# A gated complex scan with a gated feed-forward layer: the third group's running sums taken as whole 4-byte products, and three planner constants with early values

## The chip, the cores and the metric

The kernel runs on one core of one Trainium2 chip. The metric is the device time of one execution in microseconds (us), shown as the median of repeated runs. Before the change it is 616.79 us, the median of 3 runs that lie between 616.0 and 617.45.

## The reference

Inputs are `q`, `k`, `v`, `a_re` and `a_im` of shape 4 x 8 x 768 x 48 (batch, heads, time, width) and three weight matrices in 8-byte floats, 384 x 1536 twice and 1536 x 384. Cut to what matters:

```python
scale = np.minimum(mag, 0.999) / (mag + 1e-06)      # mag = |a|
for t in range(S):
    S_re, S_im = ar*S_re - ai*S_im + kv, ar*S_im + ai*S_re
    y[:, :, t] = einsum('bhd,bhde->bhe', q[:, :, t], S_re)
x = y.transpose(0, 2, 1, 3).reshape(B * S, H * D)   # 3072 x 384
g = x @ w_gate
out = (g * sigmoid(g) * (x @ w_val)) @ w_out
```

## The kernel before, in words

Time is cut into 6 chunks of 128 steps. A chunk of one batch is a slab (24 in all), and two slabs of the same chunk are a group (12, numbered 0 to 11). Each group has two halves of work.

**The scan side** (`stage_ops`, `pair_ops`). The decay of a step is turned into the logarithm of its size and its phase. Both are summed over the 128 steps of a slab by one product with a triangular matrix on TensorE (`cumulate`, L458 to 473; `cumL` sums the logarithms, `cumF` the phases). Exponentials, cosine and sine of the sums scale and turn `q` and `k`; then come scores, a mask, the product with `v` and the state that is carried on. The result is `xh` and `xl`, the rounded feed-forward input and its remainder.

**The feed-forward side** (`ffn_ops`). For each of 12 column blocks there are the products L897 (gate and value, into `p_gv`), a SiLU on ScalarE (L907), a product on VectorE (L912), and the output product L936 (into `p_po`). Group 0 takes these as whole 4-byte products, because its weights are only just converted; groups 1 to 11 take three rounded products each, of a high and a low part of both operands (type fp32r). VectorE converts the 8-byte weights in groups of three instructions (L792, L796, L800) and then splits them (L326 or L328 rounds, L322 subtracts).

**How a running sum is taken.** In groups 0 and 1 (`exact = g < 2`) `cumulate` issues one 4-byte product for each slab (L469), which runs as two TensorE instructions. From group 2 on it first calls `split`: a rounding cast (planned on VectorE or ScalarE) and a subtraction (VectorE or GpSimd) over 128 x 768 values, and then two fp32r products for each slab (L472). Since `cumulate` is called twice in a group, a split group has two casts, two subtractions and eight products; an exact group has eight TensorE instructions and no cast. The split parts borrow buffers: `LATER` puts the high and low logarithm into the buffers `s2` and `re`, those of the phase into `s1` and `s2`. For that reason the dictionary `held` (L367) makes the next group's loads and squares wait for `ls1` and `lim`, the subtractions.

**The order of the work** is not written by hand. `Planner.plan` is a list scheduler that runs when the program is built. Every operation has a key, its due time: given by `anchor` for scan slabs, by `T0`, `FT0`, `T1` and `FT` for feed-forward blocks, and handed back to what it depends on (`urge`). Whenever an engine is free in the plan, the ready operation with the smallest rank goes next. The rank is the key, plus `SWITCH_KEY` for an activation that needs another table, plus `YIELD` for an operation that VectorE could leave to another engine. `AHEAD` shifts the due times of the scan slabs. The engines then run their queues strictly in that order; before the planned time `WARM` TensorE is kept going with products of no use (L1037). `CONV0`, `CK0` and `X_SEC` give due times to weight conversions and to checks of the inputs' range.

Of the kernel before, what the change touches and what calls it, by code (L numbers as in the profile page):

```python
# [30 lines left out]

SWITCH = 1.273
HOP = 0.145
SWITCH_KEY = 2.93
STRETCH = 1.636
AHEAD, YIELD, QUEUED = -3.449, 3.533, 4.228
T0, PER, FT, FT0 = 11.002, 21.487, 3.599, 4.531
LEAD0, LEAD2 = 14.347, -0.647
CONV0, CONVP = 136.292, 171.866
T1 = T0 + 12 * FT0  # L40
CK0, CKP = 795.217, 26.993
WARM, CLEAR = 36.0, 12.0
ROW, LAND = 0.6, 2.4
SPARE, PIECE, CHECK = 0.85, 0.826, -0.265
X_SEC = 430.022
RCP, SQR, TURN, SEC = 1, 2, 4, 4
HIGH, LOW, WHOLE = 0, 1, 2
SHY = -80.37
POOL_FROM = 134.7
JOIN = 4  # L50

# [13 lines left out]
class Planner:  # L67
# [21 lines left out]
    def urge(self):  # L89
# [3 lines left out]
        for op in reversed(self.ops):  # L93
            for d in op.deps:
                span = STRETCH * max(d.engs.values()) + (0.5 * SWITCH if d.table else 0.0) + d.lat + d.move + HOP
                d.key = min(d.key, op.key - span)

    def plan(self):
        self.urge()
        free = {e: 0.0 for op in self.ops for e in op.engs}  # L100
        held = {tag: [] for tag in self.slots}
        tables, moved, shut = set(TABLES["ln"]), 0.0, 0.0
        followers, missing = {}, {}
        for op in self.ops:
            missing[op] = len(set(op.deps))
            for d in set(op.deps):
                followers.setdefault(d, []).append(op)
        loads = []
        left, order = [op for op in self.ops if not missing[op]], []
        while left:  # L110
            ready = {e: [] for e in free}
            for op in left:
                t = max([d.end + HOP for d in op.deps], default=0.0)
                for tag, _ in op.alloc:
                    if len(held[tag]) >= self.slots[tag]:
                        rel = self.released(tag, held[tag][0])
                        if rel is None:
                            t = None
                            break
                        t = max(t, rel)  # L120
                if t is None:
                    continue
                if op.move:
                    t = max(t, moved - QUEUED)
                for e in op.engs:
                    if e == "POOL" and len(op.engs) > 1 and t < POOL_FROM:
                        continue
                    ready[e].append((max(t, shut) if op.port and e in ("DVE", "POOL") else t, op))
            def rank(op):
                sw = e == "ACT" and op.table and not tables & set(TABLES[op.table])  # L130
                other = e == "DVE" and len(op.engs) > 1
                return op.key + (SWITCH_KEY if sw else 0.0) + (YIELD if other else 0.0), op.idx

            pick = None
            for e, c in ready.items():
                if c:
                    when = max(free[e], min(t for t, _ in c))
                    if e == "POOL":

                        op = min((o for t, o in c if t <= when + 0.02), key=rank)  # L140
                        if any(o.port and t <= when + 0.02 and o.key + SHY < op.key for t, o in ready.get("DVE", ())):
                            continue
                        when -= 1e-6
                    if pick is None or when < pick[0]:
                        pick = (when, e)
            if pick is None:
                raise RuntimeError("nothing can go on: " + ", ".join(o.name for o in left))
            when, e = pick
            op = min((o for t, o in ready[e] if t <= when + 0.02), key=rank)
            cost = op.engs[e]  # L150
            if e == "ACT" and op.table:

                if not tables & set(TABLES[op.table]):
                    tables = set(TABLES[op.table])
                    loads.append((op, tables))
                    cost += SWITCH
                else:
                    tables &= set(TABLES[op.table])
            for tag, inst in op.alloc:
                if len(held[tag]) >= self.slots[tag]:  # L160
                    held[tag].pop(0)
                held[tag].append(inst)
            op.start, op.eng = when, e
            free[e] = when + cost
            op.end = when + cost + op.lat
            if op.port and e in ("DVE", "POOL"):
                shut = when + cost
            if op.move:
                moved = max(moved, when + cost + 0.6) + op.move
                op.end = moved + op.lat  # L170
            order.append(op)
            left.remove(op)
            for o in followers.get(op, ()):
                missing[o] -= 1
                if not missing[o]:
                    left.append(o)
        for op, tables in loads:
            op.load = min(tables)
        return sorted(order, key=lambda o: (o.start, o.idx))


def flat(t):
    return t.rearrange("p h d -> p (h d)")
# [10 lines left out]
def quick(ctx, tc, q, k, v, a_re, a_im, w_gate, w_val, w_out, out, count):  # L194
# [81 lines left out]
    for t, (nm, f, i) in {"re": ("w", 0, 0), "im": ("w", 0, 1), "s1": ("o", 0, 0), "s2": ("w", 1, 0), "s3": ("w", 1, 1),  # L276
                          "qt": ("o", 1, 0), "kt": ("o", 2, 0), "qs": ("w", 2, 0)}.items():
        n, nm_f = 96 if t == "qs" else D, (nm, NF - 3 + f)
# [9 lines left out]
    pl = Planner(slots)  # L288
# [49 lines left out]
    def anchor(n):  # L338
        if n < 2:
            return T0 - LEAD0 + 3.0 * n  # L340
        if n < 4:
            return T0 + 4.0 + (n - 2) * 6 * FT0 - LEAD2
        return T1 + 4.0 + (n - 4) * PER - AHEAD


    def stage_ops(g, first, many):
        N = str(g) if many == 2 else f"{g}{'ab'[first]}"
        c, bp = divmod(g, 2)
        exact, lent = g < 2, g == 0
# [3 lines left out]
        def tg(t):  # L353
            at = LATER.get(t, t)
            return (("lent", at, first) if lent and t != "ks" else at), (t, g)
# [37 lines left out]
        for x, t in (("r", "s1"), ("i", "s2")):  # L393
            def square(e, x=x, t=t):
# [3 lines left out]
                else:  # L398
# [3 lines left out]
                   deps=[{"r": "ld_re", "i": "ld_im"}[x] + N, held.get(name, "")], alloc=[tg(t)], use=[tg({"r": "re", "i": "im"}[x])])  # L402
# [27 lines left out]
        def ratio(e):  # L430
            if divided:
                nc.vector.scalar_tensor_tensor(out=of("im"), in0=of("im"), scalar=-1.0, in1=of("s3"), op0=ALU.mult, op1=ALU.mult)
            else:
                nc.vector.scalar_tensor_tensor(out=of("im"), in0=of("re"), scalar=2.0, in1=of("im"), op0=ALU.subtract, op1=ALU.mult)
        pl.add("ratio" + N, STT, ratio, deps=["rec" + N, "sqi" + N] if divided else ["e1" + N, "b1" + N],
               use=[tg("s3" if divided else "re"), tg("im")], port=True)
# [20 lines left out]
        bank = "gv" if g == 0 else "pm"  # L457

        def cumulate(name, t, after):
            ins = [tg(t)]  # L460
            if not exact:
                after, ins = split(t, after)
            for i in slabs:
                inst = f"{name}{g}.{i}"

                def fn(e, i=i, inst=inst):
                    ps = new(bank, inst)[:, :HD]
                    if exact:
                        nc.tensor.matmul(out=ps, lhsT=mask, rhs=flat(half(t, i)), start=True, stop=True)  # L469
                    else:  # L470
                        for j, x in enumerate(("h" + t, "l" + t)):
                            nc.tensor.matmul(out=ps, lhsT=tri, rhs=flat(half(x, i)), start=j == 0, stop=j == 1)  # L472
                pl.add(inst, {"PE": 0.7 if exact else 0.37}, fn, deps=[after], alloc=[(bank, inst)], use=ins)

        cumulate("cumL", "s1", "l2" + N)
        for i in slabs:
            inst = f"cumL{g}.{i}"

            def exps(e, i=i, inst=inst):
                if i == first:  # L480
# [6 lines left out]
                   alloc=[] if i > first else [tg("qs")], use=[(bank, inst)] + ([tg("qs")] if i > first else []), table="exp")  # L487
        scaled = [f"exps{g}.{i}" for i in slabs]
        if c < NCH - 1:
# [6 lines left out]
            def dr2(e):  # L496
                dec = at_["dec", g] if first else new("dec", g)
                for j in range(2):
# [3 lines left out]
                   alloc=[] if first else [("dec", g)], use=[("dec", g)] if first else [], lat=5.0 if exact else 3.0 + SPARE)  # L502
# [9 lines left out]
        if c > 0:  # L512
            def cy(e):
                s = new(*tg("s"))
                for i, nm in enumerate(before):
# [3 lines left out]
                   alloc=[tg("s")], lat=2.5 + SPARE, move=1.1)  # L519
        cumulate("cumF", "im", "at" + N)  # L520
        for i in slabs:
            inst = f"cumF{g}.{i}"

            def total(e, i=i, inst=inst):
# [7 lines left out]
                else:  # L532
                    nc.vector.scalar_tensor_tensor(out=s, in0=ps, scalar=INV_2PI, in1=s, op0=ALU.mult, op1=ALU.add)
            pl.add(f"sadd{g}.{i}", STT1 if c else {"DVE": 0.47, "ACT": 0.42}, total,
                   deps=[inst, "cy" + N, "e1" + N, "b1" + N] + ([f"sadd{g}.{first}"] if i > first else []),
                   alloc=[tg("s")] if c == 0 and i == first else [],
                   use=[(bank, inst)] + ([] if c == 0 and i == first else [tg("s")]))
# [18 lines left out]
        for dst, t in (("ks", "kt"), ("qs", "qt")):  # L556
            for j, (cs, w) in enumerate(((slice(0, D), "u"), (slice(D, 96), sine))):
                opens = dst == "ks" and j == 0 and first == 0
                after = [] if opens or dst == "qs" else [f"ks0_{g}a" if first else "ks0_" + N]

                def turn(e, dst=dst, t=t, cs=cs, w=w, opens=opens):
                    if opens:
# [3 lines left out]
                       deps=["cos" + N if j == 0 else "sin" + N, "qtm" + N, "ktm" + N] + (["dr1" + N] if dst == "qs" else []) + after,  # L566
                       alloc=[tg(dst)] if opens else [], use=[tg(t), tg(w)] + ([] if opens else [tg(dst)]))
# [10 lines left out]
    def slab_ops(n):  # L578
# [81 lines left out]
        scored = dict(deps=tdeps + [f"sc{n - 1}"], alloc=[("ps", f"{n}.0"), ("ps", f"{n}.1")], use=[("T", n)])  # L660
        joined = half == 1 and n >= JOIN
        if joined:
# [191 lines left out]
    def sector_ops(g):  # L854

        N, key = f"s{g}", X_SEC + 5.0 * g
        both, parts = [(("wo", x), N) for x in range(2)], [(("ww", x), N) for x in range(2)]
# [360 lines left out]
```

## Time and profile before

| what | value |
|---|---|
| median of 3 runs | 616.79 us (616.0 to 617.45) |
| the profiled execution's own time | 616.11 us |
| its span in the profile | 614.1 us |
| PE (TensorE matmuls) busy | 595.0 us, 97% |
| DVE (VectorE) busy | 490.8 us, 80% |
| ACT (ScalarE) busy | 425.0 us, 69%, of which 119 table loads 152.7 us |
| POOL (GpSimd) busy | 39.5 us, 6% |
| granted TensorE clock, mean | 0.994 of full speed |

The span is the stretch that the profiler records; the execution's own time is 2.0 us longer. A busy share is an average: an engine can be the bound in one stretch and have slack in another, so the stretches below are read one by one. The busy time of PE is modelled for each matmul and overlaps at its ends; what a matmul takes from its engine is read from the distance of its start to the next start. In the rows, a bracket such as [1.11 <-DVE sg L912] is idle time just before the instruction and what ended it.

### The profile page before, as it was taken

What the parts mean: (1) busy time and instruction counts of PE and PEld (TensorE: products, weight loads), DVE (VectorE), ACT (ScalarE), POOL (GpSimd) and SP (SyncE); (2) the same over time, 40 slices, a digit from 0 to 9 for tenths busy, and PEclk for the clock granted to TensorE, in tenths of its full rate; (3) what the DMA queues carried; (4) which work ended last, traced back from release to release, by engine and by line L of the source; (5) the groups of instructions that cost most, each with busy time, mean ns of one, the idle gap of its engine ahead of it and who ended that gap; (6) DMA issues with size and microseconds to landing.
All of it is one profiled execution on the core that took longest, in us unless ns stands there. A gap on an engine that the chain in (4) does not pass through costs nothing.

```text
span 614.1 us, 18072 instructions
## 1 busy us (share of the span) xinstructions
PE 595.0 (97%) x7520; PEld 564.2 (92%) x7520; DVE 490.8 (80%) x892; ACT 425.0 (69%) x691; POOL 39.5 (6%) x70
## 2 busy tenths in 40 slices
PE   8789999999999999999999999999999999999995
PEld 6567778889999999999999999999999999999995
DVE  7999999999999898688688788778878868554442
ACT  7963776996865865995994994995896896213310
POOL 3210101001001000000001001001000000000000
PEclk9989999999999999999999999999999999999998
DMA  9999512443755535536545445544644643541300
GB/s 263 312 309 334 142 51 58 120 104 75 194 134 124 170 88 147 137 95 169 130 108 159 123 117 147 135 112 123 162 113 121 170 112 90 148 105 59 101 24 30
DMA packets 146279, 83.15 MB, mean 135 GB/s; under 512 B 106608, under 2 KB 142448, under 8 KB 146192
## 3 DMA queue, kind: packets, MB, share of 16 engines
q1 hardware_dynamic: 143360, 77.10, 46.7%
q0 software_dynamic: 2256, 4.06, 2.9%
q8 instruction: 61, 1.00, 0.7%
q10 hardware_dynamic: 576, 0.79, 0.4%
q14 instruction: 26, 0.21, 0.1%
HBM read 61.40 MB, written 4.78 MB: 108 GB/s over the span
## 4 chain that ended last, share of the span: by engine, by line
PE 79%; DVE 12%; ACT 4%; issue 2%; DMA 2%; SPq 0%; DVEq 0%
PE p_gv L897 42%; PE p_po L936 22%; PE p_py L701 6%; PE p_ps L658 4%; PE p_pm L707 2%; PE p_pm L472 2%; DVE xl L796 2%; DMA qt<-in_q_dram 1%; DVE ww L322 1%; ACT L1040 1%; DVE xl L792 1%; DVE sg L912 1%; DVE ww L800 1%; DVE s L322 1%; DMA ww<-in_a_re_dram 1%
## 5 line engine op out<-in xcount | busy, mean ns | idle before, releaser
L897 PE MATMUL p_gv<-xh,ww 128*128 128x256 f32 x1596 | 304.1, 288 | 3.3 <-DVE sg L912 2.6
L897 PEld LDWEIGHTS p_gv<-xh,ww 128*128 128x128 f32 x1596 | 255.6, 189 | 10.0 <-DVE sg L912 3.7
L897 PE MATMUL p_gv<-xl,ww 128*128 128x256 f32 x726 | 200.9, 277 | 0.0
L1040 ACT ACT_TABLE_LOAD x119 | 152.7, 1283 | 2.1
L897 PEld LDWEIGHTS p_gv<-xl,ww 128*128 128x128 f32 x726 | 136.4, 188 | 0.1
L936 PE MATMUL p_po<-wo,hh 128*128 128x384 f32 x484 | 124.0, 337 | 0.0
L907 ACT ACTIVATE sg<-p_gv 128x256 f32<-128x256 f32 x144 | 54.5, 384 | 91.3 <-PE p_gv L897 90.3
L912 DVE TENSOR_TENSOR sg<-sg,p_gv 128x256 f32<-128x256 f32 x144 | 59.3, 413 | 62.9 <-ACT sg L907 59.8
L936 PEld LDWEIGHTS p_po<-wo,hh 128*128 128x128 f32 x484 | 81.5, 188 | 1.1 <-issue 0.4
L936 PE MATMUL p_po<-wo,hl 128*128 128x384 f32 x242 | 81.0, 335 | 0.0
L322 DVE TENSOR_TENSOR hl<-sg,hh 128x256 fp32r<-128x256 f32 x132 | 55.0, 421 | 6.1 <-ACT hh L326 0.8
L377 ACT ACTIVATE s<-s 128x768 f32<-128x768 f32 x44 | 37.1, 844 | 12.2 <-DVE s L322 12.0
L936 PEld LDWEIGHTS p_po<-wo,hl 128*128 128x128 f32 x242 | 45.4, 188 | 0.0
L326 ACT CAST hh<-sg 128x256 fp32r<-128x256 f32 x61 | 24.7, 404 | 29.6 <-DVE sg L912 26.5
L701 PE MATMUL p_py<-sc,vt 128*32 128x128 f32 x768 | 38.6, 278 | 0.0
L672 DVE TENSOR_TENSOR sc<-p_ps,tri 128x512 f32<-128x512 f32 x48 | 31.4, 679 | 3.1 <-PE p_py L701 3.1
L658 PEld LDWEIGHTS p_ps<-T 96*32 96x32 f32 x1536 | 28.9, 111 | 5.3 <-issue 2.9
L701 PE MATMUL p_py<-T,G 96*32 96x128 f32 x640 | 33.5, 274 | 0.0
L658 PE MATMUL p_ps<-T 96*32 96x128 f32 (+3 forms) x1536 | 32.4, 235 | 0.0
L322 DVE TENSOR_TENSOR ks<-kt,s 128x768 f32<-128x768 f32 x22 | 21.0, 952 | 6.4 <-PE p_pm L707 6.4
L701 PEld LDWEIGHTS p_py<-sc,vt 128*32 128x32 f32 x768 | 24.5, 112 | 1.6 <-issue 0.8
L328 DVE CAST hh<-sg 128x256 fp32r<-128x256 f32 x71 | 21.1, 300 | 4.8 <-PE p_po L936 1.5
(145 smaller groups left out, 858.7 us busy)
## 6 DMA issues: line engine op xcount, KB each, us to landing
T<-turned SPq DMA_DIRECT2D x240, 64.0 KB, 2.1
wo<-in_moe_w_out_dram SPq DMA_DIRECT2D x24, 384.0 KB, 5.5
vt<-in_v_dram SPq DMA_DIRECT2D x24, 288.0 KB, 4.3
ww<-in_moe_w_gate_dram SPq DMA_DIRECT2D x12, 384.0 KB, 7.7
ww<-in_moe_w_val_dram SPq DMA_DIRECT2D x12, 384.0 KB, 8.6
wo<-in_moe_w_gate_dram SPq DMA_DIRECT2D x12, 384.0 KB, 3.5
wo<-in_moe_w_val_dram SPq DMA_DIRECT2D x12, 384.0 KB, 3.9
re<-in_a_re_dram SPq DMA_DIRECT2D x11, 384.0 KB, 3.7
```

Of the source, the lines that this page charges most:

```text
L322: V[e].tensor_tensor(out=out, in0=a, in1=b, op=op)
L326: nc.scalar.copy(out=out, in_=in_)
L328: nc.vector.tensor_copy(out=out, in_=in_)
L377: nc.scalar.activation(out=of(dst), in_=of(source), func=func, scale=scale, **kw)
L658: nc.tensor.matmul(out=ps[32 * slot:32 * slot + 32, at, 32 * j:P], lhsT=kT[:, h // 2, h % 2, j, :], rhs=qT[:, h // 2, h % 2, j:4, :], star ...
L672: nc.vector.tensor_tensor(out=s.rearrange("p (x h) t -> p x h t", x=2), in0=at_["ps", f"{n}.{qd}"].rearrange("p (x h t) -> p x h t", x=2, ...
L701: nc.tensor.matmul(out=o, lhsT=l, rhs=r, start=opens, stop=closes, tile_position=(0, 32 * slot))
L897: nc.tensor.matmul(out=gv[:, i, :], lhsT=l, rhs=r, start=(m == 0), stop=(m == len(mm) - 1))
L907: nc.scalar.activation(out=new("sg", I), in_=at_["gv", I][:, 0:2 * P], func=AF.Silu)
L912: nc.vector.tensor_tensor(out=sg, in0=sg, in1=at_["gv", I][:, 2 * P:4 * P], op=ALU.mult)
L936: nc.tensor.matmul(out=po, lhsT=l[:, cs], rhs=weight("o", f, part), start=f == 0 and j == 0, stop=f == NF - 1 and j == len(products) - 1)
L1040: nc.scalar.preload_act_table_set(op.load)
```

## The change

`EXACT = 3` is new: `cumulate` takes the 4-byte product for groups 0, 1 and 2, where it did so for 0 and 1. Everything else that depended on `exact` still goes by `g < 2`. Since group 2 has no split, the operations `ls1` and `lim` of group 2 do not exist, and the entries of `held` that name them for group 3 fall away. `SWITCH_KEY`, `YIELD` and `AHEAD` get second values for the early part (`EDGE = 150` in the planner's time for two of them, slabs 4 to 7 for the third), and most other constants of the planner have new values.

```diff
-SWITCH_KEY = 2.93
-STRETCH = 1.636
-AHEAD, YIELD, QUEUED = -3.449, 3.533, 4.228
-T0, PER, FT, FT0 = 11.002, 21.487, 3.599, 4.531
-LEAD0, LEAD2 = 14.347, -0.647
-CONV0, CONVP = 136.292, 171.866
+SWITCH_KEY = 2.986
+STRETCH = 1.645
+AHEAD, YIELD, QUEUED = -2.176, -1.261, 2.216
+T0, PER, FT, FT0 = -16.691, 21.329, 3.598, 4.615
+LEAD0, LEAD2 = 13.87, -1.402
+CONV0, CONVP = 236.777, 147.295
-CK0, CKP = 795.217, 26.993
+CK0, CKP = 835.905, 35.026
-SPARE, PIECE, CHECK = 0.85, 0.826, -0.265
-X_SEC = 430.022
+SPARE, PIECE, CHECK = 1.264, 0.546, 0.877
+X_SEC = 687.988
+EDGE = 150.0
+SWITCH_KEY_E, YIELD_E, AHEAD_E = 2.473, 4.357, -4.549
+EXACT = 3
...
-                return op.key + (SWITCH_KEY if sw else 0.0) + (YIELD if other else 0.0), op.idx
+                late = free["PE"] > EDGE
+                return op.key + ((SWITCH_KEY if late else SWITCH_KEY_E) if sw else 0.0) + ((YIELD if late else YIELD_E) if other else 0.0), op.idx
...
-        return T1 + 4.0 + (n - 4) * PER - AHEAD
+        return T1 + 4.0 + (n - 4) * PER - (AHEAD if n >= 8 else AHEAD_E)
...
-            if not exact:
+            if g >= EXACT:
                 after, ins = split(t, after)
...
-                    if exact:
+                    if g < EXACT:
                         nc.tensor.matmul(out=ps, lhsT=mask, rhs=flat(half(t, i)), start=True, stop=True)
...
-                pl.add(inst, {"PE": 0.7 if exact else 0.37}, fn, deps=[after], alloc=[(bank, inst)], use=ins)
+                pl.add(inst, {"PE": 0.7 if g < EXACT else 0.37}, fn, deps=[after], alloc=[(bank, inst)], use=ins)
```

## Rows read from the trace of the kernel before

**Rows 1.** The page: busy time by engine.
```profile
PE 595.0 (97%) x7520; PEld 564.2 (92%) x7520; DVE 490.8 (80%) x892; ACT 425.0 (69%) x691; POOL 39.5 (6%) x70
```

**Rows 2.** Stretches: length, busy us of PE, PEld, DVE, ACT, POOL; clock, DMA.
```profile
62.00:80.00 18.00, 18.00 (x79) 14.13 (x78) 18.00 (x31) 11.64 (x16) 2.03 (x2) 1.00 0.43 108
80.00:101.20 21.20, 20.76 (x221) 16.46 (x220) 21.20 (x37) 15.96 (x25) 2.68 (x4) 1.00 0.21 53
101.20:142.00 40.80, 38.21 (x452) 35.57 (x453) 39.27 (x72) 36.10 (x56) 2.57 (x4) 1.00 0.39 98
142.00:600.00 458.00, 457.41 (x6085) 448.82 (x6076) 352.28 (x653) 316.23 (x524) 20.17 (x33) 1.00 0.48 124
```

**Rows 3.** The chain that ended last, 131 to 134 us: start, us, what.
```profile
131.40 0.34 DVE sg L912
...
131.79 2.32 PE p_gv L897 x18
```

**Rows 4.** Timeline of TensorE: the four idle spots between 62 and 142 us.
```profile
89.62 1.62 PE L936 MATMUL p_po<-wo,sg 128*128 128x384 f32 x4 [0.44 <-DVE sg L912]
...
111.59 0.39 PE L897 MATMUL p_gv<-xh,ww 128*128 128x256 f32 x1 [1.11 <-DVE sg L912]
...
126.64 0.38 PE L897 MATMUL p_gv<-xh,ww 128*128 128x256 f32 x1 [1.08 <-DVE sg L912]
...
131.79 0.39 PE L897 MATMUL p_gv<-xh,ww 128*128 128x256 f32 x1 [0.40 <-DVE sg L912]
```

**Rows 5.** Timelines of ACT and DVE: group 2's second cast, both subtractions, next start.
```profile
75.83 0.84 ACT L326 CAST s<-im 128x768 fp32r<-128x768 f32 x1 [1.98 <-DVE re L322]
...
74.78 0.96 DVE L322 TENSOR_TENSOR re<-s,s 128x768 fp32r<-128x768 f32 x1
...
87.08 0.97 DVE L322 TENSOR_TENSOR s<-im,s 128x768 fp32r<-128x768 f32 x1
87.95 1.29 DVE L672 TENSOR_TENSOR sc<-p_ps,tri 128x512 f32<-128x512 f32 x2
```

**Rows 6.** Timeline of TensorE: an exact sum, split sums, an output product, their next starts.
```profile
29.05 0.91 PE L469 MATMUL p_pm<-s,tri 128*128 128x384 f32 x2 [0.31 <-ACT qs L485]
29.80 0.60 PE L606 MATMUL p_gv<-ident,ks 128*96 128x128 f32 x4
...
65.38 1.51 PE L936 MATMUL p_po<-wo,sg 128*128 128x384 f32 x4
66.73 2.75 PE L897 MATMUL p_gv<-xh,ww 128*128 128x256 f32 x12
...
91.43 2.75 PE L897 MATMUL p_gv<-xh,ww 128*128 128x256 f32 x12
...
133.95 0.51 PE L472 MATMUL p_pm<-s,tri 128*128 128x384 f32 x2
134.29 0.51 PE L936 MATMUL p_po<-wo,hh 128*128 128x384 f32 x2
```

**Rows 7.** Timeline of SyncE's queue: the last weight load and group 3's first load.
```profile
59.45 2.52 SPq L783 DMA_DIRECT2D ww<-in_moe_w_val_dram  x1
86.63 0.38 SPq L369 DMA_DIRECT2D re<-in_a_re_dram  x1
```

**Rows 8.** Table loads alone (length, ACT us, clock, DMA); ScalarE's timeline at 109 us.
```profile
101.20:142.00 40.80, 12.83 (x10) 1.00 0.39 98
...
109.17 1.28 ACT L1040 ACT_TABLE_LOAD   x1
110.47 0.66 ACT L907 ACTIVATE sg<-p_gv 128x256 f32<-128x256 f32 x2
```

**Rows 9.** The chain, 33 to 42 us; then VectorE's timeline, the masked scores of slab 1.
```profile
35.50 2.14 issue
...
38.87 1.82 PE p_py L701 x32
...
35.98 1.29 DVE L672 TENSOR_TENSOR sc<-p_ps,tri 128x512 f32<-128x512 f32 x2
```

## The prediction

> **What bounds the kernel now.** I read the shares of busy time first: TensorE is busy 595.0 us of a span of 614.1 [rows 1]. That is an average, so the stretches come next. From 142 to 600 us TensorE is busy 457.41 of 458.00 us while VectorE has 352.28 and ScalarE 316.23 [rows 2]: there it is the bound, and nothing that only reorders the other two can gain more than the 0.59 us that it idles. From 62 us, inside group 0's feed-forward, to 142 us it is different: VectorE is full (18.00 of 18.00, 21.20 of 21.20, 39.27 of 40.80), and TensorE is nearly full too. This is where the weights are converted and split and where group 2's scan side lies, so the change acts here. The third view, the chain of waits, says which of the two sets the pace: up to 131.74 us it runs mostly through VectorE, its last link there is the gate product L912, and from 131.79 us it stays on TensorE [rows 3]. The fourth view, TensorE's timeline, shows what VectorE's pace costs: between 62 and 142 us it idles four times, 0.44, 1.11, 1.08 and 0.40 us, each time until L912 is done [rows 4]. That is a pool of 3.03 us. After it the queue is dense, so what this part saves or adds moves the end one for one.
>
> **What goes.** Group 2 loses two casts, two subtractions and eight fp32r products. The casts ran on ScalarE, 0.84 us each [rows 5], in the 62 to 80 us stretch where ScalarE is busy 11.64 of 18.00 us [rows 2]: I cost them at nothing there, because the second one had waited 1.98 us for VectorE and nothing queued behind it set TensorE's pace. The subtractions took 0.96 and 0.97 us; the next start comes 0.87 us after the second one [rows 5]. In a full queue the two give back 2 x 0.87 = 1.74 us.
>
> **What comes.** Four 4-byte products replace four pairs, on an engine that is dense. An exact sum holds TensorE for 29.80 - 29.05 = 0.75 us [rows 6]. A split pair holds it for 134.29 - 133.95 = 0.34 us where all neighbours are fp32r [rows 6]; but group 2's pairs lie among the 4-byte products of group 0. There one pair follows an output product that starts at 89.62 us [rows 4], and the next start is 91.43; such an output product alone takes 66.73 - 65.38 = 1.35 us [rows 6], which leaves 91.43 - 89.62 - 1.35 = 0.46 us for the pair. So the addition is 4 x (0.75 - 0.46) = 1.16 us by that neighbour and 4 x (0.75 - 0.34) = 1.64 us by the other. I take 1.2, the row from the same stretch, and keep 1.6 as the upper end; that it is below nothing is excluded, since each row of a pair is under 0.75.
>
> **What moves.** Without `ls1` the buffer `re` is free once group 2's ratio is formed, so group 3's load of `a_re`, issued at 86.63 us [rows 7], no longer waits for group 2's logarithm sums. The load of `a_im` behind it gets no such lead: the exact product reads the phase itself, so the buffer `im` is held until the last phase sum and not only until the subtraction at 87.08 us [rows 5]. SyncE's queue issues nothing between the last weight load, whose issue ends at 61.97 us, and the load at 86.63 [rows 7], and from 62 to 101 us the DMA engines are busy 0.43 and 0.21 of the time [rows 2], so neither move runs into a full queue. The logarithm sums can start when the logarithm is ready instead of after cast and subtraction. These are orders of work, not work: zero in the sum, as none of TensorE's four idle spots ends on group 2's scan side; all end on L912 [rows 4]. If that cover went, a late scan would show as a wait of the scores L658.
>
> **The constants.** `CONV0` binds nothing: 136 before and 237 after are both later than any due time that a conversion inherits from group 0's products (at most `T0` + 11 x `FT0` + 3, 64 before). `CK0` and `X_SEC` rank work that fills idle time, and keep their order. `YIELD` and `SWITCH_KEY` past 150 us act where TensorE is dense: zero, covered by VectorE's 106 us and ScalarE's 142 us of slack there [rows 2]; without that cover each late SiLU would show as a gap of up to 1.1 us, as in [rows 4]. The early values (switch key 2.93 to 2.473, yield 3.533 to 4.357, slabs 4 to 7 due about 2 us later against group 0's blocks) reorder the full stretch. The trace has no row for that order, so I bound it: at best it takes out what remains of the 3.03 us and the 1.6 us that I find in the opening (below), at worst it keeps all four gaps and adds a table load.
>
> **Sum.** VectorE's path up to 131.79 us shortens by 1.74 us. TensorE's path changes by +1.2 - 3.03 = -1.8 us if all four gaps close. The later one decides: -1.7 us. Against the profiled execution (616.11 us, 2.0 more than its span) this is 614.4; that execution lies 0.7 below the median of 616.79, so the forecast is **615.1 us**, 0.28% faster. A measurement of this kernel tells some 0.2%, 1.23 us, from no change.
>
> **The rivals.**
> *A, the forecast:* the gaps close up to VectorE's 1.74. For it speaks that every gap ends on VectorE and the chain runs there. Chance 0.36; its own range is 614.2 to 616.0 (TensorE +1.6, or a gap that stays partly), of which a small part is inside 0.2%.
> *B, the opening moves too.* The first feed-forward product waits for slab 1. Before it TensorE stands still for 2.14 us, until 37.64, and then still runs useless products ahead of slab 1's product with `v`, which starts at 38.87 although its masked scores were done at 35.98 + 1.29 = 37.27 [rows 9]. A new order that avoids this gives up to 38.87 - 37.27 = 1.6 us more: 615.1 - 1.6 = 613.5. Against it: the plan cannot see that stop, and the new values may keep it. Chance 0.25.
> *C, no difference.* VectorE is relieved before 88 us, but the gaps of 111.59 and 126.64 us are made by ScalarE, which loads a table at 109.17 and does both SiLUs at 110.47 [rows 8], so only 0.44 + 0.40 us close against +1.2: 616.79 + 0.4 = 617.2. For it: ScalarE is busy 36.10 of 40.80 us in that stretch, 12.83 of it in 10 table loads [rows 2, 8]. Against it: group 3's earlier load lets some of ScalarE's work leave that stretch. Chance 0.21.
> *D, slower: ScalarE becomes the bound from 104 to 131 us.* The lower switch key makes a change of table cheaper in rank, and one more load is put ahead of a SiLU that TensorE waits for. No gap closes, TensorE's +1.2 us stays, and the load adds 1.28 us [rows 8]: 616.79 + 2.5 = 619.3; without the extra load 618.0. It decides from the point where the gaps that close are worth less than the 1.2 us. Chance 0.18. By the Trainium skill, ScalarE: Activation LUTs, section "What ACT_TABLE_LOAD costs", a switch costs a drain of some 1.38 us on top of the 1.283 us load, about 2.66 us in all; D would then be an estimated 620.7 us. The trace agrees on the load and not on the drain: the SiLU starts at 110.47, 1.30 us after the load does [rows 8].
> That `EXACT` does nothing can't be: group 2 is the only group that changes side.
>
> **How the numbers follow.** Faster by over 0.2%: nearly all of A (0.33) and nearly all of B (0.24), 0.57. Within 0.2%: C and the rest of A, 0.24. Slower by over 0.2%: D and a remainder of B's reordering gone wrong, 0.19. The range takes in B with 1.3 us for gaps that were left in A (612.2) and the middle of D (618.2), and leaves out about 2 in 10.
>
> **What would show it.** Right: the profile after has eight L469 instructions more and eight L472 fewer, VectorE and ScalarE together have four fewer, the first dense stretch of TensorE begins before 131.8 us, the idle spots ended by L912 sum to under 1.5 us, and the load of group 3's `a_re` comes well before 86 us. B: slab 1's product with `v` starts within 0.3 us of its masked scores. C or D: the gaps are still there, with a table load just ahead of the SiLU that ends them. The prediction would be wrong if TensorE idles past 142 us, which the new late `YIELD` could do, or if the end after the last output product gets longer.

## The result and the profile after

The changed kernel takes **621.77 us** (median of 5 runs, 620.84 to 622.42) against 616.0 us for the kernel before (the three runs of above and two more, 613.68 to 617.45): a ratio of 1.0092, interval 1.0073 to 1.0112. It is slower by 0.9% where 0.28% faster was forecast, outside the range. The profiled execution took 621.02 us, its span 619.0 against 614.1.

Read in the same order as before. The page's busy time by engine, of the kernel after:

```profile
PE 596.8 (96%) x7518; PEld 562.9 (91%) x7518; DVE 492.0 (79%) x894; ACT 412.8 (67%) x684; POOL 38.6 (6%) x70
```

TensorE's work hardly grew against [rows 1] (596.8 against 595.0), and ScalarE has 12.2 us less to do. No share tells where 5 us went; the stretches do. The same columns as in [rows 2], the kernel after:

```profile
62.00:80.00 18.00, 17.50 (x75) 12.86 (x74) 18.00 (x33) 11.57 (x14) 1.12 (x2) 1.00 0.50 130
80.00:101.20 21.20, 21.20 (x220) 16.56 (x220) 21.17 (x36) 17.98 (x27) 2.52 (x4) 1.00 0.21 46
101.20:142.00 40.80, 38.39 (x485) 36.25 (x484) 39.24 (x73) 36.67 (x59) 2.59 (x4) 1.00 0.37 96
...
240.00:450.00 210.00, 206.60 (x2784) 200.76 (x2774) 161.24 (x288) 160.85 (x262) 12.93 (x21) 1.00 0.54 132
```

Up to 142 us little has changed: VectorE is still full, TensorE idles about as much (2.91 us of these 80, before 3.03). The new thing is the last row. TensorE idles 3.4 us between 240 and 450 us, where VectorE and ScalarE are busy some three quarters of the time. The same window of the kernel before:

```profile
240.00:450.00 210.00, 209.41 (x2839) 205.75 (x2829) 164.82 (x300) 170.25 (x266) 12.94 (x21) 1.00 0.52 135
```

There it idled 0.59 us. TensorE's timeline of the kernel after names the spots (idle time before the instruction, and what ended it, in the bracket):

```profile
103.95 1.62 PE L940 MATMUL p_po<-wo,sg 128*128 128x384 f32 x4 [0.98 <-DVE sg L916]
...
122.84 0.38 PE L901 MATMUL p_gv<-xh,ww 128*128 128x256 f32 x1 [1.24 <-DVE sg L916]
...
254.26 0.39 PE L901 MATMUL p_gv<-xh,ww 128*128 128x256 f32 x1 [0.66 <-DVE sg L916]
...
302.02 0.39 PE L901 MATMUL p_gv<-xh,ww 128*128 128x256 f32 x1 [0.65 <-DVE sg L916]
...
349.81 0.39 PE L901 MATMUL p_gv<-xh,ww 128*128 128x256 f32 x1 [0.66 <-DVE sg L916]
...
398.04 0.38 PE L901 MATMUL p_gv<-xh,ww 128*128 128x256 f32 x1 [0.66 <-DVE sg L916]
...
445.95 0.39 PE L901 MATMUL p_gv<-xh,ww 128*128 128x256 f32 x1 [0.66 <-DVE sg L916]
```

The first two answer to [rows 4]: of four waits for the gate product between 62 and 142 us two are left, 0.98 and 1.24 us. They sum to 2.22 us, where the prediction's own sign of being right was under 1.5. Then comes a row of five, one in each of the groups 4 to 8, some 48 us apart and alike to 0.01 us: a fault of the order that repeats with the loop.

What all this is worth is read from the starts of each group's first output product in TensorE's timeline:

```text
                      before    after    after - before
first of group 0       48.45    45.64     -2.81
groups 0 and 1        111.53   113.40     +1.87
groups 2 and 3         93.04    93.36     +0.32
groups 4 to 8         234.53   240.15     +5.62
groups 9 and 10        88.94    88.95     +0.01
```

Up to group 2 the changed kernel is 0.9 us ahead, all of it from the opening; groups 0 and 1, where the whole products lie, take 1.9 us more. Groups 4 to 8 lose 5.6 us, 1.1 us each, and that is the result. A wait that shows as 0.66 us of idle time costs more than itself: the last output product before it starts at 253.26 and would have made room at 253.44, so the product at 254.26 is 0.82 us late. The next product starts 0.22 us behind it where 0.11 is usual, and the product at 260.64, which waits for the fourth SiLU (259.75), loses another 0.2 us in the same way.

**Why the gate product is late there.** ScalarE's timeline of the kernel after, ahead of the spot at 254.26:

```profile
247.54 1.28 ACT L1044 ACT_TABLE_LOAD   x1
248.84 0.39 ACT L911 ACTIVATE sg<-p_gv 128x256 f32<-128x256 f32 x1
249.24 1.28 ACT L1044 ACT_TABLE_LOAD   x1
250.53 0.85 ACT L381 ACTIVATE s<-s 128x768 f32<-128x768 f32 x1
251.29 0.39 ACT L330 CAST hh<-sg 128x256 fp32r<-128x256 f32 x1
251.58 0.47 ACT L330 COPY ost<-p_po 128x384 f32<-128x384 f32 x1
252.07 1.28 ACT L1044 ACT_TABLE_LOAD   x1
253.36 0.66 ACT L911 ACTIVATE sg<-p_gv 128x256 f32<-128x256 f32 x2
```

and VectorE's, which waits for it:

```profile
253.78 0.75 DVE L916 TENSOR_TENSOR sg<-sg,p_gv 128x256 f32<-128x256 f32 x2 [0.32 <-ACT sg L911]
```

Between the first SiLU of the group and the second, the planner has put the logarithm of a later group (L381 at 250.53). It costs two table loads, one there and one back, and the second SiLU starts at 253.36. TensorE wanted its gate product at 253.44. The kernel before had at the same place:

```profile
248.87 0.39 ACT L907 ACTIVATE sg<-p_gv 128x256 f32<-128x256 f32 x1
...
250.20 0.39 ACT L907 ACTIVATE sg<-p_gv 128x256 f32<-128x256 f32 x1
...
257.69 1.28 ACT L1040 ACT_TABLE_LOAD   x1
258.98 0.38 ACT L907 ACTIVATE sg<-p_gv 128x256 f32<-128x256 f32 x1
```

The first and the second SiLU followed each other in one table, 1.33 us apart, and the loads came later, one SiLU at a time. The gate products of the second and the fourth SiLU in VectorE's timeline there, and the products in TensorE's that need their banks (the result buffers that a gate product frees):

```profile
250.87 0.41 DVE L912 TENSOR_TENSOR sg<-sg,p_gv 128x256 f32<-128x256 f32 x1
...
259.40 0.42 DVE L912 TENSOR_TENSOR sg<-sg,p_gv 128x256 f32<-128x256 f32 x1 [2.50 <-ACT sg L907]
```

```profile
254.06 0.28 PE L897 MATMUL p_gv<-xh,ww 128*128 128x256 f32 x1
...
260.22 0.28 PE L897 MATMUL p_gv<-xh,ww 128*128 128x256 f32 x1
```

The second one's was done at 250.87 + 0.41 = 251.3 us and used at 254.06: 2.8 us of cover (the time from the end of what is waited for to its use). In the kernel after that SiLU follows the first by 4.52 us, 3.2 us more, and the cover is gone. The fourth SiLU, at 258.98, had less: its gate product was done at 259.40 + 0.42 = 259.8 and used at 260.2, a cover of 0.4 us.

**The opening** [rows 9] started 2.8 us earlier in this execution, though the stop is still there (2.32 us, from 35.59). The granted clock differs: windows of the kernel before, then of the kernel after, columns as in [rows 2],

```profile
37.00:39.00 2.00, 1.36 (x9) 1.13 (x12) 2.00 (x5) 0.47 (x2) 1.26 (x2) 0.53 1.13 315
39.00:41.00 2.00, 2.00 (x68) 1.87 (x63) 0.93 (x2) 1.17 (x3) 0.41 (x1) 0.62 1.17 223
```

```profile
37.00:39.00 2.00, 1.09 (x30) 0.97 (x33) 2.00 (x4) 0.79 (x2) 0.73 (x1) 1.00 1.21 237
39.00:41.00 2.00, 2.00 (x65) 1.86 (x58) 1.44 (x3) 1.84 (x4) 0.77 (x2) 1.00 1.03 310
```

show it at 0.53 and 0.62 before and at 1.00 after. Another kernel below (run 2) with the same order up to there has 0.83 and 0.50 in these two windows. From the end of the stop to the first output product it takes 47.55 - 38.24 = 9.31 us, and the kernel after 45.64 - 37.91 = 7.73, so some 1.6 of the 2.8 us belong to that execution's clock and not to the change.

### The profile page after: what moved, and what is told of

Same layout as the page of the kernel before. It is cut to its first block, busy times and chain, and to the rows that moved or that the text cites. A ratio compares the mean times of both kernels' runs of the same rounds, so it can differ in the third digit from the quotient of the medians.

```text
span 619.0 us, 18040 instructions
## 1 busy us (share of the span) xinstructions
PE 596.8 (96%) x7518; PEld 562.9 (91%) x7518; DVE 492.0 (79%) x894; ACT 412.8 (67%) x684; POOL 38.6 (6%) x70
## 4 chain that ended last, share of the span: by engine, by line
PE 67%; ACT 12%; DVE 9%; issue 5%; DMA 5%; SPq 1%; ACTq 0%; DVEq 0%
PE p_gv L901 35%; PE p_po L940 18%; PE p_py L705 6%; ACT L1044 5%; PE p_ps L662 4%; ACT s L381 3%; DMA wo<-in_moe_w_out_dram 2%; PE p_pm L476 2%; PE p_pm L711 2%; ACT sg L911 1%; DMA re<-in_a_re_dram 1%; SPq L787 1%; DVE sg L916 1%; DVE xl L800 1%; DVE ww L326 1%
## 5 line engine op out<-in xcount | busy, mean ns | idle before, releaser
L330 ACT CAST hh<-sg 128x256 fp32r<-128x256 f32 x74 | 29.8, 403 | 34.3 <-DVE sg L916 21.0
L381 ACT ACTIVATE s<-s 128x768 f32<-128x768 f32 x44 | 37.1, 844 | 10.3 <-DVE s L326 9.2
L662 PE MATMUL p_ps<-T 96*32 96x64 f32 (+3 forms) x1536 | 32.6, 235 | 0.2 <-DVE T L332 0.2
L735 ACT CAST xh<-p_py 128x384 fp32r<-128x384 f32 x22 | 10.5, 477 | 21.1 <-PE p_py L705 21.0
L901 PE MATMUL p_gv<-xh,ww-1_369 128*128 128x256 f32 x132 | 24.6, 279 | 0.0
```

What stands on the lines that cost most here:

```text
L330: nc.scalar.copy(out=out, in_=in_)
L381: nc.scalar.activation(out=of(dst), in_=of(source), func=func, scale=scale, **kw)
L662: nc.tensor.matmul(out=ps[32 * slot:32 * slot + 32, at, 32 * j:P], lhsT=kT[:, h // 2, h % 2, j, :], rhs=qT[:, h // 2, h % 2, j:4, :], star ...
L901: nc.tensor.matmul(out=gv[:, i, :], lhsT=l, rhs=r, start=(m == 0), stop=(m == len(mm) - 1))
```

## The experiments

Theory (called W in some expectations): the loss is the late SiLU of groups 4 to 8, because ScalarE's order has no slack at that place. The main rival: the whole products, or the early part, cost it.

**1. The constants alone** (group 2 split as before):

```diff
-EXACT = 3
+EXACT = 2
```

> The changed kernel with group 2 split again (EXACT = 2), all new constants kept. Theory W (the loss is one wait of TensorE per group in groups 4 to 8, made by the order that the late constants give ScalarE): the order in those groups is the same, so five idle spots of 0.65 us ended by the gate product remain and the time is 620 to 624 us. Rival X (the whole products cost it, on TensorE or by what they move): 616 to 618 us.

Measured: 624.43 us, ratio 1.0135 (1.011 to 1.016). The five spots of 0.66 us are there, at 257.30 to 450.56. So they come from the constants and not from the whole products. The time is 0.4 us above the range of theory W, as new waits stand beside them, the longest 2.31 us at 111.94. The excess over the kernel before is 8.3 us here and 5.8 us with whole products. That does not price the products: groups 0 and 1, where they lie, take 113.5 us here and 113.4 in the kernel after, and groups 2 to 8, which the planner ordered anew, 335.7 and 333.5.

**2. The SiLU before the logarithm**: in groups 4 to 8 the second SiLU and the cast `hh` are moved ahead of the logarithm on ScalarE.

```diff
+    for g in range(4, 9):
+        ahead(f"th_{g}.1", f"lnm{g + 2}")
+        ahead(f"hh_{g}.0", f"lnm{g + 2}")
```

> The changed kernel, its order kept, except that in groups 4 to 8 the second SiLU and the first rounding cast of the group stand ahead of the logarithm that stood between the first two SiLUs on ScalarE. Theory W: the five waits go, 5 x 1.27 us (the period is 47.8 us with the wait and 46.5 without), 615 to 617 us. Rival X: nothing that matters moves, 620.5 to 622.5 us.

A miss, above both ranges: 624.06 us, ratio 1.0127 (1.01 to 1.0154). TensorE's timeline of this kernel, the first of five pairs:

```profile
252.75 0.39 PE L901 MATMUL p_gv<-xh,ww 128*128 128x256 f32 x1 [0.18 <-DVE sg L916]
263.08 0.38 PE L901 MATMUL p_gv<-xh,ww 128*128 128x256 f32 x1 [0.38 <-DVE sg L916]
```

The wait of 0.66 us is gone and two others have come. The two loads did not vanish; they moved ahead of the next SiLUs, which had no slack either. So it isn't one activation in a wrong place: this order asks ScalarE for too much around each of those SiLUs.

**3. Whole products alone**: the order of before, group 2's casts and subtractions left out, whole products in it, the load of `a_im` right behind the last phase sum that reads its buffer.

```diff
-                    if exact:
+                    if g < 3:
...
+    order = [op for op in pl.plan() if op.name not in ("hs12", "ls12", "him2", "lim2")]
+    later = pl.by["ld_im3"]
+    order.remove(later)
+    order.insert(order.index(pl.by["cumF2.1"]) + 1, later)
```

> The kernel before with its order kept; group 2's two casts and two subtractions are left out and its sums are whole 4-byte products; group 3's load of the phase follows group 2's last phase sum. The prediction's sum: 1.74 us off VectorE, 1.2 us onto TensorE, up to 3.0 us of idle spots to close: 614 to 616 us. ScalarE theory (the idle spots end on table loads, not on VectorE): TensorE's 1.2 us stays, 616.5 to 618 us. Rival X: 620 us or more.

Measured: 619.33 us, ratio 1.0052 (1.0028 to 1.0075): slower, so the forecast's sum has the wrong sign here. TensorE's timeline of this kernel:

```profile
78.46 1.52 PE L936 MATMUL p_po<-wo,sg 128*128 128x384 f32 x4
79.82 0.81 PE L469 MATMUL p_pm<-s,tri 128*128 128x384 f32 x2
...
95.02 0.81 PE L469 MATMUL p_pm<-im,tri 128*128 128x384 f32 x2
...
97.10 1.08 PE L701 MATMUL p_py<-sc,vt 128*32 128x128 f32 x32
...
105.98 0.60 PE L936 MATMUL p_po<-wo,sg 128*128 128x384 f32 x1 [0.85 <-DVE wo L800]
...
114.71 0.39 PE L897 MATMUL p_gv<-xh,ww 128*128 128x256 f32 x1 [1.81 <-DVE sg L912]
```

The order is the same as before, so the block between the same two products can be compared: 97.10 - 78.46 = 18.64 us without an idle spot, against 95.81 - 77.64 = 18.17 us with the 0.44 us of [rows 4] in it. The four whole products cost 18.64 - 17.73 = 0.91 us, and the gap closed. But behind it stand 0.85 us that were not there, and 1.81 in place of 1.11. VectorE did not use what it was relieved of: it is busy 18.05 of the 21.20 us from 80 us, where it had been full [rows 2]. ScalarE's timeline shows why:

```profile
99.22 0.84 ACT L397 ACTIVATE s<-im 128x768 f32<-128x768 f32 x1 [3.62 <-DMA im<-in_a_im_dram]
99.97 0.88 ACT L326 CAST ww<-ww 128x768 fp32r<-128x768 f32 x1
100.75 0.84 ACT L377 ACTIVATE s<-s 128x768 f32<-128x768 f32 x1
```

It stands 3.62 us before the load of `a_im`, with a weight cast and the sine behind it on its queue. That load was issued at 95.91, after the last phase sum, and 7.8 us later than before (88.13); 0.8 us of that is this execution's later opening.

**4. The phase sums side by side**: as 3, but the second phase sum right behind the first, and the load right behind both.

```diff
-    order.insert(order.index(pl.by["cumF2.1"]) + 1, later)
+    at = "cumF2.0"
+    for name in ["cumF2.1", "ld_im3"]:
+        later = pl.by[name]
+        order.remove(later)
+        order.insert(order.index(pl.by[at]) + 1, later)
+        at = name
```

> The order of before with whole products in group 2, as in the earlier run of that kind, but group 2's last phase sum stands right behind the first one, and group 3's load of a_im right behind both. In the earlier run ScalarE waited 3.62 us for that load until 99.22 us, and TensorE then waited 0.85 and 1.81 us at 105.98 and 114.71. Theory 1: the late load makes these two waits, since the whole product holds the buffer of the phase until the last sum. Then the load is issued near 93.2 instead of 95.9 us, ScalarE's square starts near 96.6, the first wait falls under 0.3 and the second to 1.1 to 1.4 us, and the time is 617.4 to 618.5 us. Theory 2: the whole products themselves make the waits, since TensorE and what reads the sums are later by their length. Then both waits stay within 0.2 us of 0.85 and 1.81, and the time is 618.9 to 619.8 us.

Measured: 618.11 us, ratio 1.0031 (1.0014 to 1.0048), as by theory 1. ScalarE waits 1.25 us for the load in place of 3.62, the wait of 0.85 us is gone, that of 1.81 is 1.22. What is left of the loss, 1.7 us against this comparison's 616.41, is the 0.9 us of products and a wait of 0.65 us that this edit makes itself (at 91.97 the second sum waits for a bank). The later waits, 1.22, 1.08 and 0.32 us, are those of [rows 4] again: without two subtractions of VectorE they did not close.

**5. One table load**: the kernel before, with one needless load ahead of the second SiLU in groups 4 to 8.

```diff
+            if op.name in [f"th_{g}.1" for g in range(4, 9)]:
+                nc.scalar.preload_act_table_set("silu_and_others")
```

> The kernel before with one needless table load (1.28 us of ScalarE) ahead of the second SiLU of groups 4 to 8, nothing else changed. If what covers ScalarE is the slack of the whole stretch (142 us), no difference: 615.5 to 617. Theory W (the cover is local): the fourth SiLU's gate product is done at 259.8 us and the sixth gate and value product of the group could start at about 260.2, so 0.4 us is covered and 0.9 us a group is not: 5 x 0.9 = 4.4 us, 619 to 622 us.

Measured: 621.3 us, ratio 1.0094 (1.0068 to 1.012), as much as the whole change. TensorE's timeline, the first of five new spots:

```profile
261.69 0.40 PE L897 MATMUL p_gv<-xh,ww 128*128 128x256 f32 x1 [0.42 <-DVE sg L912]
```

1.28 us more in a stretch of 47 us in which ScalarE idles some 9 us in each group (170.25 busy of 210 us from 240 us on) costs TensorE 4.1 us over the five groups (238.6 against 234.5). The place it costs is not where the load stands, where the cover was 2.8 us, but two SiLUs later, where it was 0.4 us.

**6. The loads taken out**: the kernel after, with the logarithm of groups 6 to 10 in place of `Ln` as a function that needs no table.

```diff
-        act("lnm", "s1", "s1", AF.Ln, "ln", ["m2"])
+        act("lnm", "s1", "s1", AF.Square if 6 <= g <= 10 else AF.Ln, "ln", ["m2"])
...
+    for g in range(6, 11):
+        pl.by[f"lnm{g}"].table = None
```

> The changed kernel with its order kept; for groups 6 to 10 the logarithm of the squared size is replaced by a square, which every table holds (the recurrence's decays are then not the reference's). ScalarE does the same number of activations but needs no table for this one, so 2 x 1.28 us of loads go from each of the five places between the first two SiLUs of groups 4 to 8. Theory W (ScalarE's order there makes TensorE wait): no wait and no small bubble is left in groups 4 to 8, the period falls from 47.8 to 46.5 us, 5 x 1.27 = 6.3 us in all, 614.5 to 617.5 us (the opening varies by some 2 us between executions). If the waits come from VectorE, or from the loads and transfers: 620 to 622.5 us.

Measured: 617.38 us, ratio 1.0014 (0.9997 to 1.0032). No gate product is waited for in groups 4 to 8, which take 235.9 us in place of 240.2. With the loads go 4.2 of the 5.6 us. Of the 1.4 us that stay in these groups, one wait of 0.62 us at 330.68, for `xl` from VectorE, is a part; the rest is not explained.

**7. A copy to VectorE**: the kernel after, with the copy `ost` (0.47 us at 251.58) on VectorE in groups 4 to 8.

```diff
+    for g in range(4, 9):
+        pl.by[f"oe{g - 1}.1"].eng = "DVE"
```

> The changed kernel with its order kept; the copy of an output block that stands between the first two SiLUs of groups 4 to 8 runs on VectorE instead of ScalarE (0.47 us less for ScalarE each). Theory W: TensorE's wait there shrinks by about 0.47 us, five times, so 2.4 us less than the changed kernel: 618.5 to 620.5 us, and the recorded idle spot falls from 0.66 to 0.2 us. Rival (VectorE is what is late): 0.55 us more each time, 622 to 625 us.

Measured: 620.27 us, ratio 1.007 (1.0046 to 1.0095). The five spots shrink from 0.66 to 0.28 us, by nearly what the copy took, and groups 4 to 8 take 238.6 us in place of 240.2. TensorE's timeline of this kernel, the first of the five:

```profile
255.98 0.39 PE L901 MATMUL p_gv<-xh,ww 128*128 128x256 f32 x1 [0.28 <-DVE sg L916]
```

**8. The late values put back**: the kernel after with the old switch key, yield and shift past the edge.

```diff
-SWITCH_KEY = 2.986
+SWITCH_KEY = 2.93
-AHEAD, YIELD, QUEUED = -2.176, -1.261, 2.216
+AHEAD, YIELD, QUEUED = -3.449, 3.533, 2.216
```

> The changed kernel with the late values of the switch key, the yield and the lead put back (2.93, 3.533, -3.449); early values and whole products kept; the planner makes a new order past 150 us. Theory W in its simple form (these values alone spoil the late part): no repeated wait, 614 to 617 us. If instead any new order of the late part has little slack on ScalarE, as the planner prices activations too low, waits stay in other places: 618 to 623 us.

Measured: 621.24 us, ratio 1.0078 (1.0053 to 1.0104). The row of five is gone, but others stand elsewhere, TensorE's timeline of this kernel:

```profile
215.76 0.38 PE L901 MATMUL p_gv<-xh,ww 128*128 128x256 f32 x1 [0.78 <-DVE sg L916]
...
446.95 0.38 PE L901 MATMUL p_gv<-xh,ww 128*128 128x256 f32 x1 [1.00 <-DVE sg L916]
```

So putting these three values back is not enough: groups 2 to 8 together take 333.6 us, against 333.5 in the kernel after and 327.6 before. In both rows a table load stands just ahead of the late SiLU again (213.58 and 444.77), so an order that puts a load too close to a SiLU comes about in more than one way.

**9. Fewer useless products in the opening**: the kernel before with `WARM` at 31 in place of 36, ten TensorE instructions fewer.

```diff
-WARM, CLEAR = 36.0, 12.0
+WARM, CLEAR = 31.0, 12.0
```

> The kernel before without its last ten useless instructions on TensorE (the filling ends at 31 us instead of 36). They run for 1.23 us after the stop at 35.5 us and before slab 1's product with v. If the stop stays, that product starts 1.2 us earlier and the time falls by 1 to 1.3 us: 614.8 to 615.2 us where before is 616.1. If the stop or a lower granted clock behind it takes up what is gained: no difference, 615.5 to 617 us.

Measured: 614.82 us, ratio 0.9979 (0.9964 to 0.9994). Slab 1's product with `v` starts at 37.23 in place of 38.87, as rival B had it, then TensorE stops again for 0.57 us, and the first output product starts at 48.5 as before. The median gains 1.6 us, in the first range of the expectation, but the profiled execution is the slowest of the ten (617.0 us), so it doesn't show where the gain comes from.

**10, 11, 12. Orders made for the durations of the trace**: the planner with a price of its own for a table load (`TABLE`), activations at the trace's durations, and constants chosen so that no gate product comes late when the order is replayed with those durations. One set with whole products, the same set with group 2 split, and a set chosen for the split. The first:

```diff
+TABLE, ACT0, ACT1 = 1.337, 0.138, 0.251
-SWITCH_KEY = 2.986
+SWITCH_KEY = 3.449
-AHEAD, YIELD, QUEUED = -2.176, -1.261, 2.216
+AHEAD, YIELD, QUEUED = -2.194, 6.565, 4.228
-T0, PER, FT, FT0 = -16.691, 21.329, 3.598, 4.615
+T0, PER, FT, FT0 = 11.002, 21.469, 3.594, 4.483
-EDGE = 150.0
-SWITCH_KEY_E, YIELD_E, AHEAD_E = 2.473, 4.357, -4.549
+EDGE = 139.064
+SWITCH_KEY_E, YIELD_E, AHEAD_E = 2.054, 3.533, -3.45
...
-                    cost += SWITCH
+                    cost += TABLE
...
-    table = {"ACT": 0.15 + 0.27 * x, "DVE": 0.07 + 0.4 * x, "DVE2": 0.07 + 0.2 * x, "POOL": 0.1 + 0.86 * x}
+    table = {"ACT": ACT0 + ACT1 * x, "DVE": 0.07 + 0.4 * x, "DVE2": 0.07 + 0.2 * x, "POOL": 0.1 + 0.86 * x}
```

> The changed kernel (whole products in group 2, early and late constants) with other values for the planner's constants, and other prices for a table load and an activation. They are chosen so that, when every step of the resulting order is charged with the time that the traces show for it on ScalarE (0.75 us between starts of two 768-column activations, 1.29 us for a table load and 0.11 us more for the activation before it), no gate product of groups 3 to 10 comes after the product that needs its bank. Theory W, with the cause in the order and not in the whole products: no repeated wait past 140 us, fewer idle spots before it, 608 to 613 us. If a whole product in group 2 costs what the fixed order showed (3 us) in any order: 614 us or more.

Measured: 618.23 us, ratio 1.0035 (1.002 to 1.005), a miss. The late part is clean: groups 4 to 8 take 234.5 us, as before the change, without a repeated wait. The early part gives it back (groups 0 and 1 take 114.9 us, before 111.5), so this run does not exclude the expectation's second case, that whole products cost something in any order. TensorE's timeline of this kernel:

```profile
51.69 0.64 PE L611 MATMUL p_gv<-ident,qs 128*96 128x128 f32 x4 [2.46 <-DVE sg L917]
```

> The kernel of the run retuned_whole with EXACT = 2, so that group 2 is split again; the same constants. If whole products in group 2 are good by themselves: slower than retuned_whole by 1 us or more throughout. If they are bad by themselves: faster. Charged with the trace's durations this order ends 4.7 us later than that of retuned_whole, of which the order's luck is a part that this run can't separate: 611 to 617 us.

Measured: 623.41 us, ratio 1.0119 (1.0096 to 1.0142), a miss as well. The same constants give another order when group 2 is split, and this one is worse by 5.2 us; what part of that the whole products have is not shown.

> The kernel of the run retuned_whole with a set of constants of its own, chosen in the same way for a split group 2 (EXACT = 2). If the gain over the kernel before is in the order alone and the whole products add little: 609 to 613 us, and not more than 2 us behind retuned_whole. If the whole products are what makes the gain: 615 us or more.

Measured: **613.72 us**, ratio 0.9956 (0.9939 to 0.9973), faster than both kernels. That is 0.7 us above the first range and 4.5 us ahead of the set for whole products, which neither case of the expectation had. It has the switch key at 3.049, late yield 7.693 and group 2 split. Groups 4 to 8 take 233.9 us. Its lead over the kernel before, 2.4 us of span, is in the opening (first output product at 46.28, 2.2 us earlier); groups 0 to 10 gain 0.6 us together, and the end gives 0.3 back. TensorE's timeline of this kernel, and then a window of it:

```profile
37.14 1.08 PE L706 MATMUL p_py<-sc,vt 128*32 128x128 f32 x32 [1.17 <-DVE sc L677]
```

```profile
39.00:41.00 2.00, 1.43 (x7) 1.31 (x8) 2.00 (x4) 0.97 (x3) 0.00 (x0) 1.00 0.89 134
```

The stop "issue" is absent: TensorE waits for the masked scores, and slab 1's product starts with them, as rival B described. The clock stays at 1.00.

## Why the prediction was wrong

- **The step that failed:** "`YIELD` and `SWITCH_KEY` past 150 us act where TensorE is dense: zero, covered by VectorE's 106 us and ScalarE's 142 us of slack there". The slack was counted over 458 us. At the places that count, the SiLUs on which TensorE's next block hangs, the kernel before had 2.8 us at the second of group 4 and 0.4 us at the fourth, and run 5 bears this out: a load of 1.28 us cost 4.1 / 5 = 0.8 us in each group. Measured: +5.6 us in groups 4 to 8, of which 4.2 go with the logarithm's table loads (run 6). Which constants made that order is not shown. The sum has no word for the other constants that also order the late part (`PER`, `STRETCH`, `QUEUED`, the late `AHEAD`). The condition that the text names for being wrong, TensorE idling past 142 us, came about, but had no term in the sum and no chance of its own. Rival D had the mechanism, a load ahead of a SiLU, at the wrong place and once in place of five times.
- **What comes, right with a size off:** the four whole products cost 0.91 us against 1.2 taken and 1.6 as the upper end (run 3). The price from the same stretch was the better neighbour.
- **What goes, wrong:** the 1.74 us of subtractions were to pull the gaps shut. In the fixed order they closed only the first, 0.44 us; the other three stayed (run 4). VectorE runs its queue in order, so what it is spared ahead of a wait it spends in that wait: in run 4 it is busy 18.25 of the 21.20 us from 80 us. The chain of [rows 3] ran mostly through VectorE, but a link ahead of the last two gaps was ScalarE's, in VectorE's timeline of the kernel before:

```profile
121.05 0.96 DVE L322 TENSOR_TENSOR ww<-ww,ww 128x768 fp32r<-128x768 f32 x1 [0.95 <-ACT ww L326]
```

Run 4 has the same wait, 0.91 us. Rival C had the outcome, gaps that stay, but its reason only in part: at 111.59 the SiLU was done 0.27 us before VectorE came to it (110.85 and 111.12), and at 126.64 it was done 1.1 us before (125.09 and 126.18).
- **What moves, half right:** the load of `a_re` is issued at 68.41 in place of 86.63. "The load of `a_im` behind it gets no such lead" was seen and costed at nothing. In a fixed order it is 7.8 us later; placing it sooner saved 1.2 us (run 3 against 4, whose own wait for a bank is in that). The new order avoids this by taking group 2's phase sums first (75.47 and 78.14 us), which lets that load go at 79.13.
- **Counts:** eight L469 more (L473 in the kernel after), eight L472 fewer (there L476), and VectorE with ScalarE four fewer apart from one table load (1578 against 1583): right.
- **The early sum, wrong:** up to group 2 the kernel is 0.9 us ahead, against 1.7 forecast, but by an opening that the sum did not have, and most of that opening's 2.8 us is that execution's clock. Runs 2, 6 and 7 have the same early order and reach group 2's first output product at 161.06, 159.77 and 160.66 us, against 159.98 in the kernel before: no gain. Had the late part stayed at zero, the median would be 621.77 - 5.62 = 616.2 us by estimate, the time of the kernel before.
- **The range:** the middle of D's two times, 618.0 and 619.3, is 618.7 and not 618.2. The measured time lies above either.
- Rival D's page: the Trainium skill, ScalarE: Activation LUTs, section "What ACT_TABLE_LOAD costs", adds a drain of some 1.38 us to a switch of tables. The rows here do not show one: the copy ahead of the load ends at 252.05, the load begins at 252.07, and the next SiLU starts 1.29 us later, at 253.36. So a load is dear here by its place and not by its length.

**Open:** which of the constants makes the late order. Run 8 shows only that putting three of them back does not undo the loss. An order that has both the clean late part and a good early part with whole products was not found, so whether whole products can pay off here is not settled: in the fixed order they cost 1.7 to 3.2 us, and the fastest kernel here has group 2 split.

## What to carry to other kernels

Count slack at the place, not over the stretch: for each thing that the bound engine (the one that sets the pace) waits for, take the time from its end to its use, and ask what the new order puts ahead of it. Where a planner orders the work, a change of its constants is a change of the whole order; look for idle spots that repeat with the loop's period, since a wait of half a microsecond in each turn outweighs what a local saving brings. An engine relieved of work in a strict queue finishes sooner only if nothing that it waits for further on stays where it was.

## What was not expected of the hardware

- TensorE stops for 2.0 to 2.6 us, from a time between 35.0 and 36.3 us on, with "issue" as the only cause, in 12 of the 14 kernels profiled here. The DMA share is above 1 then (1.06 to 1.21 from 35.5 to 38 us), but so it is in the fastest kernel (1.07), which has no such stop; the cause stays open. Afterwards the granted clock is at or near the lower level (1.2 GHz) in 10 of the 12. Run 2's windows have

```profile
37.00:39.00 2.00, 0.76 (x10) 0.52 (x13) 2.00 (x4) 0.78 (x2) 0.66 (x1) 0.83 1.21 183
39.00:41.00 2.00, 2.00 (x54) 1.85 (x49) 0.51 (x1) 0.51 (x2) 0.84 (x2) 0.50 1.01 318
```

and the kernel after, with the same order and a stop of 2.32 us in place of 2.61, stays at 1.00. Between the two lie 1.9 us in the first output product (47.55 and 45.64). Single profiles therefore differ by about 2 us in the opening alone, and only the medians of several runs compare.
- At a full granted clock TensorE has patches in which its products start some 4% further apart. In the kernel before, twelve of them take 255.53 - 254.17 = 1.36 us, and in a patch later on 396.67 - 395.26 = 1.41 us. Its timeline:

```profile
254.17 0.28 PE L897 MATMUL p_gv<-xl,ww 128*128 128x256 f32 x1
...
255.53 0.28 PE L897 MATMUL p_gv<-xl,ww 128*128 128x256 f32 x1
```

```profile
395.26 0.28 PE L897 MATMUL p_gv<-xl,ww 128*128 128x256 f32 x1
...
396.67 0.28 PE L897 MATMUL p_gv<-xl,ww 128*128 128x256 f32 x1
```

What makes these patches is not shown.
